# Loading w_down's last row of each partition by eight loads of four partitions

## The chip, the cores and the metric

The kernel runs on one core of a Trainium2 chip. The metric is the device time of one execution in microseconds (us). A core has engines that run side by side, each with its own queue of instructions: TensorE (PE; its weight loads are listed as PEld), VectorE (DVE), ScalarE (ACT), GpSimd (POOL) and SyncE (SP). In this kernel SP issues all transfers between device memory and the on-chip memory of 128 partitions; 16 DMA engines carry them out.

## What is computed

One decoding step of four sequences: attention over a cache of 4096 positions and 32 heads, a gated feed-forward net beside it, and a mix of the two by a gate. All of it is in float32.

```python
g = sigmoid((x * gate_w).sum(-1, keepdims=True))          # x: 4 x 1 x 512
q = x @ wq                                                # wq: 512 x 4096, 32 heads of 128
p = softmax(q @ k_cache.T * 128 ** -0.5)                  # k_cache: 4 x 32 x 4096 x 128
a = (p @ v_cache) @ wo                                    # wo: 4096 x 512
b = (gelu(x @ w_gate) * (x @ w_up)) @ w_down              # 512 x 1792, 512 x 1792, 1792 x 512
out = g * a + (1 - g) * b
```

The two caches are 256 MiB each, and nearly all of the kernel's traffic. wq and wo are 8192 KB each, w_gate, w_up and w_down 3584 KB each.

## The kernel before

**Stages.** At the start wq, x, the first K tile and gate_w are loaded, then w_gate and w_up. The queries are computed on PE. The loop over `i` in 0 to 31 then takes one K tile and one V tile a step: four heads of one sequence, 8192 KB each, 64 KB in each partition. DVE multiplies a K tile by the query (`products`, L213) and sums over the head's 128 elements (`sums`, L219), each in two parts: a quarter of the tile that is shared with its neighbour in memory first, and then the other three quarters. PE turns the maxima (L228, L235), ACT takes the exponentials (L240), and PE multiplies the result by V(i-1) (`pv`, L272). In step 0 the feed-forward net up to its hidden vector is computed as well: `ffn_up` on PE (L334), `ffn_gelu` on DVE and ACT (L341 to L346), and 14 transposes of 128 by 32 on DVE (L349) into `hT`. After the loop come `load_d` (w_down, one load, L88) and `load_w` twice (wo, two loads of 2048 KB for its first half and six of 1024, 1024, 768, 512, 512 and 256 KB for its second, L95). PE then runs the last `pv`, the product with w_down (`ffn_down`, 14 products through `project_wide`, L254), the first half of wo (also L254), the fold of `wide` into `acc` (L264, L259) and the second half of wo (L259, four products for each of 16 rows, as its pieces land). DVE copies the result (L413) and SP stores it (L414).

**Memory.** One tile `big` of 45056 floats in each partition holds everything large. Even K tiles are in columns 0 to 16383, odd ones in 12288 to 28671, so neighbours share a quarter. V tiles are in 28672 to 45055, the last one, V(31), in 0 to 16383. w_down is put in 36864 to 44031 and the first half of wo in 28672 to 36863, both once V(30) has been used by PE; the second half of wo is put in 16384 to 24575, once K(31) has been summed by DVE. The columns 24576 to 26623, also in K(31), serve small results (`ES`).

**Order.** The schedule is by hand: each engine executes its instructions in the order of the program text, and a framework adds the semaphores. SP's order near the end is K(31), V(30), V(31), w_down, then wo in eight pieces, then the store. An SP instruction that waits holds all that are behind it.

Of the kernel before, what the change touches and what calls it, by code (L numbers as in the profile page):

```python
# [9 lines left out]
F32 = mybir.dt.float32  # L10
# [7 lines left out]
def tile_gated_mix(ctx: ExitStack, tc: tile.TileContext, x, kc, vc, wq, wo, w_gate, w_up, w_down, gate_w, out):  # L18
    nc = tc.nc
    P = 128  # L20
    B, H, S, D = kc.shape
    DM = x.shape[2]
    F = w_gate.shape[1]
# [9 lines left out]
    RJ = 4  # L33
    BP = 2
    FG = F // 4
    FC = F // P
    HW = 16
    E = HW * D // P
    GW = HW // HT
# [12 lines left out]
    consts = ctx.enter_context(tc.tile_pool(name="consts", bufs=1))  # L52
# [9 lines left out]
    big = kv.tile([P, VA + TW], F32)  # L62
    Q0, F0, F1, W0, D0 = VA, VA, VA + KC * F, VA, VA + TW // 2
    W1, ES = TW, TW + TW // 2

    def place(a, n):
        return big[:, a:a + n]
# [17 lines left out]
        nc.sync.dma_start(place((F0, F1)[s], KC * F), (w_gate, w_up)[s].rearrange("(p c) n -> p (c n)", c=KC))  # L85

    def load_d():
        nc.sync.dma_start(place(D0, FC * DM), w_down.rearrange("(p i) n -> p (i n)", i=FC))  # L88

    def load_w(w):  # L90
        t = place((W0, W1)[w], E * DM)
# [152 lines left out]

    acc = ps1.tile([P, C4], F32, name="acc")
    wide = ps1.tile([P, DM], F32, name="wide")
    NW = FC + E
    nw = iter(range(NW))


    def project_wide(t, w):
        n = next(nw)
        c = n % 4
        nc.tensor.matmul(wide[32 * c:32 * c + 32, :], t, w, start=n < 4, stop=n >= NW - 4)  # L254

# [69 lines left out]


    hT = consts.tile([P, FC, 32], F32)
    fu = place(VA + 2 * KC * F, 2 * DM).rearrange("p (s n) -> p s n", s=2)

    def ffn_up(s):  # L330
# [7 lines left out]
    def ffn_gelu():  # L338
        x1 = fu[:, 0, :FG]
        t1, t2, t3, th, y, v = (place(F1 + a * DM, FG) for a in range(6))  # L340
        nc.vector.tensor_tensor(t1, x1, x1, op=OP.mult)  # L341
        nc.vector.tensor_scalar(t2, t1, 0.044715, 1.0, op0=OP.mult, op1=OP.add)
        nc.vector.tensor_tensor(t3, t2, x1, op=OP.mult)  # L343
        nc.scalar.activation(th, t3, AF.Tanh, scale=c_gelu)  # L344
        nc.vector.scalar_tensor_tensor(y, th, 1.0, x1, op0=OP.add, op1=OP.mult)  # L345
        nc.vector.scalar_tensor_tensor(v, y, half, fu[:, 1, :FG], op0=OP.mult, op1=OP.mult)  # L346

        for i in range(FC):
            nc.vector.transpose(hT[:, i, :], v[:, i::FC])  # L349

    def ffn_down():
        for f in range(FC):
            project_wide(hT[:, f, :], place(D0 + f * DM, DM))


    load_f(0)
# [2 lines left out]
    for i in range(NT):  # L359
# [12 lines left out]
        if i == 0:  # L372
            half, gmask = gates()
            ffn_up(0)
            ffn_up(1)
            ffn_gelu()
            load_v(0)
# [14 lines left out]
        if b == 1 and g + 1 < NG:  # L392
            q_spread(g + 1)
    load_d()
    load_w(0)
    load_w(1)
# [4 lines left out]
    gather(NG - 1)  # L401
    weigh(NG - 1)
    ffn_down()
    turn(1)
    turned(1)
# [31 lines left out]
```

## Time and profile before

| what | value |
|---|---|
| median of 3 runs (lowest, highest) | 1313.7 us (1313.62, 1313.85) |
| the profiled execution | 1313.51 us |
| its span in the profile | 1311.7 us |
| DVE busy | 1143.1 us, 87% |
| PE busy | 392.2 us, 30% |
| ACT busy | 92.6 us, 7% |
| mean granted clock of TensorE | 0.633 |

The profile covers one execution; what lies between its span and its time, 1.8 us, is ahead of the first instruction and behind the last. Rows have the start and the duration in microseconds, the engine, the source line and operation, and the tile written and the tiles read ("big<-in_A_wo" is a load of wo into `big`). SPq is SP's queue. In the chain of waits each row is a stretch of the work that ended last, followed back from the end; a stretch put down to a DMA runs from its issue, or from the end of the row before it, to its landing. In lists of waits the columns are the waiting engine and line, what it waited for, the sum, the number of waits and the longest. A wait for several things is put down to the one that the profile saw last. In rows by line, "|" is followed by the busy time and the mean duration in nanoseconds, and then by the idle time before. Rows of stretches give the bounds, the length, busy time and instructions of PE, PEld, DVE, ACT and POOL, then the granted clock, the share of the DMA engines' time and GB/s.

### The profile page before, as it was taken

To read this page: it belongs to the slowest core of one execution; us is meant where nothing else is said; L and a number is where in the kernel's file an instruction comes from. 1 tells how busy PE (TensorE), PEld (TensorE's weight loads), DVE (VectorE), ACT (ScalarE), POOL (GpSimd) and SP (SyncE) were. 2 spreads that over 40 slices of the span, in tenths; PEclk is the share of its full clock that TensorE was granted. 3 is DMA by queue.
4 is the path that set the end of the run, shared out by engine and by line. 5 is a ranking of instruction groups with operands and counts; after the bars stand their busy time and mean duration, and the time that the engine had idled before them with its cause. 6 is when DMAs were issued, how large, how long until landed. Compare 5 with 4: busy or idle time off the path is not lost.

```text
span 1311.7 us, 6366 instructions
## 1 busy us (share of the span) xinstructions
PE 392.2 (30%) x2728; PEld 131.1 (10%) x2728; DVE 1143.1 (87%) x261; ACT 92.6 (7%) x321; POOL 0.7 (0%) x6
## 2 busy tenths in 40 slices
PE   2403323322233221333232233322133333123237
PEld 0100001000010000100001000100001000010013
DVE  1899889988899988988989988998889898898890
ACT  0010000000000100000000000000000000000010
POOL 0000000000000000000000000000000000000000
PEclk9656666556666655666656666665566665566669
DMA  9999999999999999999999999999999999999998
GB/s 416 436 428 442 422 440 426 438 436 436 436 428 436 432 436 436 436 430 432 434 436 434 436 430 436 428 438 430 434 446 422 442 422 442 434 434 440 426 426 341
DMA packets 11143, 565.07 MB, mean 431 GB/s; under 512 B 1368, under 2 KB 1384, under 8 KB 1900
## 3 DMA queue, kind: packets, MB, share of 16 engines
q1 hardware_dynamic: 11116, 564.68, 99.5%
q8 instruction: 21, 0.34, 0.1%
q14 instruction: 6, 0.05, 0.0%
HBM read 564.67 MB, written 0.01 MB: 430 GB/s over the span
## 4 chain that ended last, share of the span: by engine, by line
DMA 73%; DVE 26%; issue 0%; PE 0%; SPq 0%; ACT 0%; DVEq 0%
DMA big<-in_A_k_cache 69%; DVE big L213 13%; DVE sc L219 13%; DMA big<-in_A_v_cache 2%; DMA big<-in_A_wo 2%; DVE m L233 0%; DVE hT L349 0%; PE acc L259 0%; DVE big L346 0%; DVE big L345 0%; DVE big L341 0%; DVE big L343 0%; ACT big L344 0%; DVE m L226 0%; DVE t L313 0%
## 5 line engine op out<-in xcount | busy, mean ns | idle before, releaser
L213 DVE TENSOR_TENSOR big<-big,qb 128x4096 f32<-128x4096 f32 x64 | 555.8, 8685 | 104.1 <-DMA big<-in_A_k_cache 104.1
L219 DVE TENSOR_REDUCE sc<-big 128x32 f32<-128x4096 f32 x64 | 555.4, 8678 | 1.1
L272 PE MATMUL po<-big,PM 128*32 128x512 f32 x2048 | 295.1, 741 | 437.2 <-DMA big<-in_A_v_cache 434.8
L272 PEld LDWEIGHTS po<-big,PM 128*32 128x32 f32 x2048 | 80.9, 133 | 625.2 <-issue 622.7
L235 PE MATMUL sm<-m,ones 1*128 1x4 f32 x64 | 18.7, 360 | 218.0 <-DVE m L233 218.0
L228 PE MATMUL sm<-ident,m 128*1 128x128 f32 x32 | 11.7, 365 | 214.5 <-DVE m L226 182.7
L240 ACT ACTIVATE PM<-sc,nb 32x128 f32<-32x128 f32 x128 | 67.3, 526 | 2.5
L237 ACT ACTIVATE nb<-sm 128x4 f32<-128x4 f32 x32 | 5.5, 173 | 570.3 <-PE sm L235 570.3
L235 PEld LDWEIGHTS sm<-m,ones 1*128 1x128 f32 x64 | 15.9, 306 | 237.7 <-DVE m L233 237.7
L281 ACT ACTIVATE o<-po 128x512 f32<-128x512 f32 x16 | 9.6, 597 | 324.8 <-PE po L272 324.8
L228 PEld LDWEIGHTS sm<-ident,m 128*1 128x1 f32 x32 | 2.5, 79 | 237.0 <-issue 185.9
L240 ACT ACTIVATION_READ_ACCUMULATOR PM<-sc,nb 32x1 f32 x128 | 26.2, 205 | 0.0
L200 ACT ACTIVATE qb<-q 128x512 f32<-128x512 f32 x8 | 4.8, 597 | 245.3 <-PE q L196 245.3
L128 DVE COPY xT<-sm 128x128 f32<-128x128 f32 x4 | 0.9, 284 | 20.6 <-PE sm L125 20.6
L196 PE MATMUL q<-QM,hmask 128*32 128x512 f32 x64 | 14.6, 1004 | 3.5 <-DVE QM L186 3.5
L289 PE MATMUL sm<-o,sel 128*16 128x128 f32 x128 | 15.6, 273 | 0.0
L334 PE MATMUL q<-big,xT 128*32 128x448 f32 x64 | 10.3, 810 | 9.4 <-DMA big<-in_B_w_gate 4.9
L299 DVE RECIPROCAL ri<-sm 16x1 f32<-16x1 f32 x8 | 1.2, 146 | 13.3 <-PE sm L291 13.3
L289 PEld LDWEIGHTS sm<-o,sel 128*16 128x16 f32 x128 | 11.8, 97 | 7.4 <-issue 5.0
L413 DVE COPY res<-acc 128x128 f32<-128x128 f32 x1 | 0.3, 291 | 12.7 <-PE acc L259 12.7
L226 DVE TENSOR_REDUCE m<-sc 128x1 f32<-128x128 f32 x32 | 9.2, 286 | 1.1
L233 DVE TENSOR_REDUCE m<-sm 1x4 f32<-1x128 f32 x32 | 8.7, 272 | 0.6 <-PE sm L228 0.6
(61 smaller groups left out, 77.1 us busy)
## 6 DMA issues: line engine op xcount, KB each, us to landing
big<-in_A_wo SPq DMA_DIRECT2D x2, 2048.0 KB, 27.0
big<-in_B_w_gate SPq DMA_DIRECT2D x1, 3584.0 KB, 21.4
big<-in_B_w_up SPq DMA_DIRECT2D x1, 3584.0 KB, 27.5
big<-in_B_w_down SPq DMA_DIRECT2D x1, 3584.0 KB, 18.0
big<-in_A_wo SPq DMA_DIRECT2D x2, 1024.0 KB, 24.6
big<-in_A_wo SPq DMA_DIRECT2D x2, 512.0 KB, 28.2
big<-in_A_wo SPq DMA_DIRECT2D x1, 768.0 KB, 28.0
big<-in_A_k_cache SPq DMA_DIRECT2D x32, 29.6
```

Source lines behind the costliest of these rows:

```text
L196: nc.tensor.matmul(ps[h * PH:(h + 1) * PH].rearrange("p b d -> p (b d)"), hmask[:, j, a:a + 1].to_broadcast([P, PH]), QM.rearrange("p b d ...
L213: nc.vector.tensor_tensor(t, t, QB[g][:, b:b + 1, :].to_broadcast([P, r1 - r0, D]), op=OP.mult)
L219: nc.vector.tensor_reduce(SC[i][:, r0:r1], K(i).rearrange("p (r d) -> p r d", d=D)[:, r0:r1], axis=AX.X, op=OP.add)
L226: nc.vector.tensor_reduce(m1, SC[i], axis=AX.X, op=OP.max)
L228: nc.tensor.transpose(MT[i], m1, ident)
L233: nc.vector.tensor_reduce(m2, MT[i].rearrange("o (h p) -> o h p", h=HT), axis=AX.X, op=OP.max)
L235: nc.tensor.matmul(nbp, ones[:1, :], m2, start=True, stop=True)
L240: nc.scalar.activation(PM[:, PZ:].rearrange("p (c m) -> p c m", m=32)[s, :, h:RJ * HT:HT], SC[i][s, :].rearrange("p (c j) -> p c j", j=RJ) ...
L272: nc.tensor.matmul(PO[i // BP % 2][32 * c:32 * c + 32].rearrange("p j d -> p (j d)"), PM[:, m0:m0 + 32], V(i)[:, j * N:(j + 1) * N], start ...
L281: nc.scalar.activation(O[i // BP], PO[i // BP % 2], AF.Copy)
L289: nc.tensor.matmul(OS[g][:, :D], sel[:, j, m0:m0 + B * HT], O[N * g + n][:, j, :], start=(n, j) == (0, 0), stop=(n, j) == (N - 1, RJ - 1))
L334: nc.tensor.matmul(ps[32 * j:32 * j + 32, :], xT[:, c, :32], place((F0, F1)[s] + c * F + j * FG, FG), start=c == 0, stop=c == KC - 1)
```

## The change

w_down's 1792 rows lie 14 to a partition. Thirteen of each partition's 14 are still loaded by one load, now into 6656 instead of 7168 columns. The last row of each of the 128 partitions, 128 rows of 2 KB in all, goes to partitions 0 to 31 instead, four rows to a partition, in columns 26624 to 28671 (`DX`), by eight loads. Load `p` writes the partitions p, p+8, p+16 and p+24 and carries 16 rows, 32 KB. The hidden vector is transposed to match: 13 transposes as before and four of 32 by 32 into `hX`. The product with w_down becomes 13 products over 128 partitions and four over 32. The numbers that are summed are the same.

```diff
-    FC = F // P
+    FR = F // P
+    FC = FR - 1
+    XP, XC = 32, P // 32
...
+    DX = ES + 4 * DM
...
     def load_d():
-        nc.sync.dma_start(place(D0, FC * DM), w_down.rearrange("(p i) n -> p (i n)", i=FC))
+        rows = w_down.rearrange("(p i) n -> p i n", i=FR)
+        nc.sync.dma_start(place(D0, FC * DM), rows[:, :FC].rearrange("p i n -> p (i n)"))
+        last = rows[:, FC].rearrange("(k a p) n -> p a k n", k=XC, p=8)
+        for p in range(8):
+            nc.sync.dma_start(place(DX, XC * DM)[p:XP:8].rearrange("a (k n) -> a k n", k=XC), last[p])
...
-    NW = FC + E
+    NW = FC + XC + E
...
     hT = consts.tile([P, FC, 32], F32)
+    hX = consts.tile([XP, XC, 32], F32)
...
         for i in range(FC):
-            nc.vector.transpose(hT[:, i, :], v[:, i::FC])
+            nc.vector.transpose(hT[:, i, :], v[:, i::FR])
+        for k in range(XC):
+            nc.vector.transpose(hX[:, k, :], v[k * XP:(k + 1) * XP, FC::FR])
...
     def ffn_down():
         for f in range(FC):
             project_wide(hT[:, f, :], place(D0 + f * DM, DM))
+        for f in range(XC):
+            project_wide(hX[:, f, :], place(DX + f * DM, DM)[:XP])
```

## The prediction

> **What bounds the kernel now.** I read the page's totals first, then the chain of waits in order of time, then the waits and the issue times of SyncE's DMA queue (SP) near the end.
>
> ```profile
> span 1311.7 us, 6366 instructions
> PE 392.2 (30%) x2728; PEld 131.1 (10%) x2728; DVE 1143.1 (87%) x261; ACT 92.6 (7%) x321; POOL 0.7 (0%) x6
> DMA  9999999999999999999999999999999999999998
> q8 instruction: 21, 0.34, 0.1%
> HBM read 564.67 MB, written 0.01 MB: 430 GB/s over the span
> big<-in_B_w_down SPq DMA_DIRECT2D x1, 3584.0 KB, 18.0
> ```
>
> The DMA engines are busy in every slice, VectorE (DVE) for 87%. The bytes set the time; what counts is whether the DMA queue ever runs empty. The chain shows the same, and its rhythm gives a price:
>
> ```profile
> 1202.71 4.42 DVE big L213
> ...
> 1241.31 4.42 DVE big L213
> ...
> 1250.28 29.67 DMA big<-in_A_v_cache
> ...
> 1279.97 27.61 DMA big<-in_A_wo
> ...
> 1307.62 1.08 PE acc L259 x24
> ...
> 1308.72 0.29 DVE res L413
> ```
>
> One step of the loop is 1241.31 - 1202.71 = 38.6 us for one K and one V load of 8192 KB each: 19.3 us for 8192 KB behind other loads. The last wait is for wo:
>
> ```profile
> 1308.23 0.16 PEld L259 LDWEIGHTS acc<-big 128*32 128x32 f32 x8 [0.23 <-DMA big<-in_A_wo]
> ```
>
> So the last piece of wo lands at 1308.2, and 3.5 us of work end the span. Every microsecond by which that landing moves is a microsecond of the kernel. Now the queue that issues these loads:
>
> ```profile
> SPq L95 <- DMA big<-in_B_w_down: 8.1, 1, 8.1
> SPq L95 <- DVE m L226: 4.8, 1, 4.8
> SPq L95 <- DMA big<-in_A_v_cache: 2.1, 1, 2.1
> 1270.41 0.33 SPq L88 DMA_DIRECT2D big<-in_B_w_down  x1
> 1270.79 0.43 SPq L95 DMA_DIRECT2D big<-in_A_wo  x1
> 1276.13 0.33 SPq L95 DMA_DIRECT2D big<-in_A_wo  x1
> 1279.97 0.33 SPq L95 DMA_DIRECT2D big<-in_A_wo  x1
> 1288.43 0.33 SPq L95 DMA_DIRECT2D big<-in_A_wo  x1
> ```
>
> After V(31) come w_down and eight pieces of wo. Neither of the last two pieces shares memory with what it waits for: the seventh waits for V(31), which lands at 1279.97, the eighth for w_down, which lands at 1288.43. In both cases the awaited load is the one eight places before it in the queue's order. I read this as a limit: each load reuses the completion counter of the load eight before it, and SP holds it, and everything behind it, until that one has landed. Today this costs nothing: seven of the eight pieces stand in the queue long before w_down lands, and only the last, 256 KB, comes late.
>
> **The change part by part.** *The queue.* Eight small loads (32 KB each, 256 KB together) now stand between w_down and wo. Their place is columns 26624 to 28671, the end of K(31). The sum at L219 reads that until
>
> ```profile
> 1263.15 12.95 DVE L219 TENSOR_REDUCE sc<-big 128x96 f32<-128x12288 f32 x1
> ```
>
> 1276.10, so the first small load goes out at 1276.1, where the third piece of wo goes out now (the 4.8 us wait above). The first two pieces of wo, issued from 1270.79 now, are held behind it. That alone would be free: V(31) and w_down keep the DMA engines fed until about 1287.8, and without this cover it would cost up to 1276.1 - 1270.8 = 5.3 us.
>
> The eight before are another matter. The seventh small load is eight places behind V(31) and waits until 1279.97. The eighth is eight places behind w_down and waits for its landing. All of wo stands behind that eighth load. So none of wo's 8192 KB can be issued until the last byte of everything before it has landed: the queue runs empty once. What is late next is wo's last landing, and with it the end.
>
> The price, step by step. w_down loses one row in 14, 256 KB; at 430 GB/s that is 262144 B / 430 GB/s = 0.6 us, so it lands at 1288.43 - 0.6 = 1287.8. The eighth small load is issued then. The trace has no load of its shape (4 partitions by 4 rows); the nearest rows are the load of x, of four partitions, and the store of the result, of four by four runs:
>
> ```profile
> L99 SPq DMA_DIRECT2D big<-in_A_x x1: 355/355/355, 1.2 to 1.2; - x1
> L414 SPq DMA_DIRECT2D out<-res x1: 661/661/661, 1309.0 to 1309.0; - x1
> L97 SPq DMA_DIRECT2D big<-in_A_wq x1: 388/388/388, 0.7 to 0.7; - x1
> DMA to landing us min/median/max: 21.9/21.9/21.9
> ```
>
> That is 0.36 to 0.66 us; I take 0.55, between them, and 0.05 to the next issue (1270.79 - 1270.41 - 0.33). The first piece of wo goes out at 1287.8 + 0.6 = 1288.4, within 1288.2 to 1288.5.
>
> What do 8192 KB take from issue to last landing when the queue is empty? The trace has exactly one such load, wq (512 x 4096 floats, 8192 KB), the kernel's first: 21.9 us, the last row above. That is 21.9 - 19.3 = 2.6 us more than behind other loads: start-up, refill and the last receipts. wo in eight pieces takes 1308.2 - 1288.4 = 19.8 us from w_down's landing now, 0.5 more than the loop's 19.3; whether that half microsecond comes again bounds wo at 21.9 to 22.4. I take 22.4, since the pieces stay as they are. wo's last landing: 1288.4 + 22.4 = 1310.8, that is +2.6 against 1308.2.
>
> The Trainium skill (DMA: Bandwidth & Descriptors, Anatomy of one DMA) gives a fixed cost of about 2.0 us per DMA, nearly all of it the receipt after the last byte, fitted on GpSimd's path. By that figure an empty queue would cost 2.0 instead of 2.6 and the sum would be smaller by 0.6; the trace's row is of this queue and this size, so it decides.
>
> One more term is small but not nothing. The page's queue q8 fetches instructions over the same DMA engines, 21 packets for 2728 + 2728 = 5456 TensorE instructions, or 260 instructions each.
>
> ```profile
> 590.98 30.69 DMA big<-in_A_k_cache
> ...
> 630.67 29.67 DMA big<-in_A_k_cache
> ...
> 1094.68 30.69 DMA big<-in_A_k_cache
> ...
> 1134.37 29.59 DMA big<-in_A_k_cache
> 1288.40:1308.20 19.80, 14.95 (x226) 7.55 (x221) 1.74 (x4) 1.82 (x3) 0.00 (x0) 1.00 0.87 365
> ```
>
> The tail has 226 + 221 = 447 of these, so one or two fetches. In the loop two K landings of some 29 come late, by 30.69 - 29.6 = 1.1 us. I estimate that a fetch delays the engine it strikes by up to this, and that in steady state most fetches strike an engine that is not the last. After an empty queue all engines start level, so a strike in wo's 20 us can count in full: 0 to 1.1, I take 0.5, about the middle.
>
> *VectorE.* Fourteen transposes become thirteen and four smaller ones:
>
> ```profile
> 68.46 1.71 DVE L349 STREAM_TRANSPOSE hT<-big 128x32 f32<-128x32 f32 x14
> 70.31 0.33 SPq L76 DMA_DIRECT2D big<-in_A_v_cache  x1
> 50.97 0.33 SPq L76 DMA_DIRECT2D big<-in_A_k_cache  x1
> DMA to landing us min/median/max: 25.8/29.6/40.4
> ```
>
> 1.71 / 14 = 0.12 each: +0.4 if a smaller one costs as much, -0.1 if next to nothing. They hold up V(0)'s issue at 70.31, but K(1), issued at 50.97 and landed at 50.97 + 25.8 = 76.8 at the earliest (the last row is the time from issue to landing of all K and V loads), still feeds the DMA engines. Nothing, or +0.4 if that cover were gone.
>
> *TensorE.* Fourteen products of w_down become seventeen, four of them over 32 partitions.
>
> ```profile
> L254 PE MATMUL wide<-big,hT 128*32 128x512 f32 x28 | 3.6, 595 | 0.0
> 1298.35 0.16 PEld L254 LDWEIGHTS wide<-big 128*32 128x32 f32 x8 [2.30 <-DMA big<-in_A_wo]
> ```
>
> 3.6 / 14 = 0.26 each at most, so +0.8, or +0.3 if a product over 32 partitions costs little. PE waits 2.3 us for wo right afterwards, which hides it; bare it would be +0.8. The last small load must be there too: issued at 1287.8, it lands within 2 us if the result's store is a guide (issued 1309.04, all over at 1311.7), while the products begin at 1290.4.
>
> The sum: wo's last landing -0.6 (smaller w_down) + 0.6 (issues) + 2.6 (empty queue) + 0.5 (a fetch) = **+3.1**; the rest is hidden. The profiled execution took 1313.51, of which the span is 1311.7; it lies 0.2 below the median of the runs, 1313.7. So 1316.6 for an execution like it and **1316.8** for the median. The bounds: 0.36 + 0.05 for the issues, 21.9 for wo, no fetch, gives 1310.1 and 1315.6; 0.71, 22.4 and 1.1 gives 1312.0 and 1317.5.
>
> **The rivals.** *A: no empty queue, not slower.* The two waits at L95 could be something other than a limit of eight in flight, such as an ordering by memory that I don't see. Then the eighth small load goes out at about 1280, wo follows from 1280.5, seven microseconds before the DMA engines are through, and the bytes are the same as before: 1313.7, or down to 1313.1 if the small loads run on DMA engines that are ahead of the others and only w_down's 0.6 shows. For it: such a limit stands nowhere in the kernel's text. Against it: two waits in a row, each on the load eight places before.
>
> *B: a quarter of the engines.* A load of four partitions may be carried by four DMA engines only. Then 256 KB at a quarter of 430 GB/s take 2.4 us on those four, which save 0.6 of w_down: +1.8 at wo's landing, without an empty queue: 1315.5. The Trainium skill (DMA: Bandwidth & Descriptors, Why a DMA increments its semaphore by 16 and not by 1) says so: the number of engines is the largest up to 16 that divides the slowest dimension, four here. No view of this profile tells the engines apart. With the empty queue this hides in it: seven of the loads are through in 7 x 0.3 = 2.1 us after w_down.
>
> *C: both.* If those four engines are also the last to finish w_down, they start wo up to 2.4 - 1.5 = 0.9 us after the others (1.5 being the gap, estimated as the 0.6 of issues and about 1 us to the first byte out of wq's 2.6): 1317.7.
>
> **How the numbers follow.** The forecast, 1315.6 to 1317.5, gets 0.75, C 0.10, A 0.08 and B 0.07. No change that this kernel's measurement could tell ends at 0.2%, 2.6 us: below 1311.1 or above 1316.3. About two thirds of the forecast's own range and C lie above: 0.75 x 0.68 + 0.10 = 0.61 slower. The rest of the forecast, A and B are within: 0.37. For faster, which none of the cases gives, 0.02. The range 1315.0 to 1318.2 leaves out A and a remainder.
>
> **What would show it.** The eighth small load and all eight pieces of wo issued after 1287.5, with a wait of SP on w_down of about 7 us at the new load's line; the slices or a window of 1284 to 1290 with a visible drop of the DMA share; wo's last landing near 1311.3. wo issued near 1280.5 would prove A or B. The forecast is wrong if the refill after an empty queue in mid-kernel costs much less than at the program's start, or if a fetch falls clear of wo.

## The result, and the profile after

The changed kernel takes 1324.22 us (median of 6 runs, 1323.33 to 1324.9) against 1313.7 before: 1.0079 times as long, with a 95% interval of 1.0066 to 1.0092. That is +10.5 us. The prediction was +3.1 and a range that ended at 1318.2. The profiled execution took 1323.63, its span is 1321.8, against 1313.51 and 1311.7.

The page's totals of the changed kernel hardly differ from those before; only the last slices of the DMA row do.

```profile
span 1321.8 us, 6396 instructions
PE 390.5 (30%) x2734; PEld 131.3 (10%) x2734; DVE 1143.9 (87%) x264; ACT 92.5 (7%) x321; POOL 0.7 (0%) x6
DMA  9999999999999999999999999999999999999986
```

The waits of SP's queue over the last 97 us (waiting line and what it waited for, sum, times, longest) and SP's own timeline there (start, duration):

```profile
SPq L97 <- DMA big<-in_B_w_down: 7.8, 1, 7.8
SPq L97 <- DVE m L235: 5.5, 1, 5.5
```

```profile
1270.99 0.33 SPq L94 DMA_DIRECT2D big<-in_B_w_down  x1
1276.49 13.31 SPq L97 DMA_DIRECT2D big<-in_B_w_down  x8
1289.85 3.98 SPq L104 DMA_DIRECT2D big<-in_A_wo  x8
```

This is the predicted step. The first small load goes out at 1276.49. The eighth waits 7.8 us for w_down and goes out at 1289.17 (the chain below). All eight pieces of wo follow from 1289.85 on. The DMA engines do run dry. The same stretch before and after (bounds, length, busy time and count of PE, PEld, DVE, ACT, POOL, granted clock, DMA share, GB/s), first the kernel before:

```profile
1284.00:1290.00 6.00, 6.00 (x61) 2.34 (x50) 0.00 (x0) 0.60 (x1) 0.00 (x0) 1.00 0.97 414
```

and the changed kernel:

```profile
1284.00:1290.00 6.00, 0.00 (x0) 0.00 (x0) 0.00 (x0) 0.00 (x0) 0.00 (x0) 0.50 0.36 121
1313.00:1319.00 6.00, 5.11 (x148) 3.78 (x140) 0.11 (x1) 0.60 (x1) 0.00 (x0) 1.00 0.01 3
```

The DMA share falls from 0.97 to 0.36. But the first row shows something else as well: TensorE, busy for all of these 6 us before, does nothing. And in the second row all loads are through by 1313, while TensorE works on for 6 us. The end no longer follows wo's landing. The chain of the changed kernel, in order of time, says what it follows (left out rows are marked by "..."):

```profile
1270.99 18.16 DMA big<-in_B_w_down
...
1289.17 2.54 DMA big<-in_B_w_down
...
1291.97 0.63 ACT big L329
1292.60 0.07 ACT nb L246
...
1294.90 8.37 PE po L281 x64
1303.27 1.77 PE sm L298 x16
...
1314.91 3.96 PE acc L268 x136
...
1318.89 0.29 DVE res L427
```

The eighth small load lands at 1291.71. Only then does ScalarE run L329, the copy of `spread(0)`, and behind it in its program order the softmax of the last tile and with it the last `pv`, the gather and everything that TensorE does to the end. ScalarE's timeline at that copy (in brackets the idle time before and who ended it), before:

```profile
1276.14 0.63 ACT L320 ACTIVATE big<-t 128x512 f32<-128x512 f32 x1 [27.18 <-DVE sc L219]
```

and after:

```profile
1291.97 0.63 ACT L329 ACTIVATE big<-t 128x512 f32<-128x512 f32 x1 [42.65 <-DMA big<-in_B_w_down]
```

Before, the copy waits for VectorE's last sum. After, it waits for the small loads, 15.8 us longer. The last `pv` starts at 1294.90; before, it started at 1280.35:

```profile
1280.35 8.39 PE L272 MATMUL po<-big,PM 128*32 128x512 f32 x64 [2.45 <-ACT PM L240]
```

The copy writes columns 24576 to 25087, the loads write 26624 to 28671: they share nothing. The order that the framework made of the program nevertheless lists all eight loads' counters ahead of the copy:

```
L329 Activation big<-t 128x512 [waits DMAHW4, DMAHW3, DMAHW5, DMAHW2, DMAHW6, DMAHW1, DMAHW7, DMAHW0, DVE]
```

From `pv` to the result's copy it is 24.0 us now (1318.89 - 1294.90). Before it was 28.4 (1308.72 - 1280.35), waits for wo included. So of `pv`'s delay of 14.55 us, 4.4 are absorbed by waits that are no longer there, and 10.2 remain: the change.

### The profile page after: what moved, and what is told of

It reads as the page before. It is cut to its first block, busy times and chain, and to the rows that moved or that the text cites. A ratio compares the mean times of both kernels' runs of the same rounds, so it can differ in the third digit from the quotient of the medians.

```text
span 1321.8 us, 6396 instructions
## 1 busy us (share of the span) xinstructions
PE 390.5 (30%) x2734; PEld 131.3 (10%) x2734; DVE 1143.9 (87%) x264; ACT 92.5 (7%) x321; POOL 0.7 (0%) x6
## 4 chain that ended last, share of the span: by engine, by line
DMA 73%; PE 23%; DVE 2%; issue 0%; ACT 0%; SPq 0%; ACTq 0%; DVEq 0%
DMA big<-in_A_v_cache 69%; PE po L281 22%; DMA big<-in_A_k_cache 3%; DMA big<-in_B_w_down 2%; DVE big L222 1%; PE wide L263 1%; DVE sc L228 0%; PE acc L268 0%; ACT PM L249 0%; PE sm L298 0%; DVE hT L359 0%; PE oT L316 0%; DVE hX L361 0%; DVE big L356 0%; DVE big L355 0%
## 5 line engine op out<-in xcount | busy, mean ns | idle before, releaser
L173 PE MATMUL po<-big,xT 128*32 128x512 f32 x64 | 9.0, 729 | 0.4 <-DVE xT L137 0.4
```

## The experiments

The theory from these rows: two costs, ScalarE held behind the small loads and the empty queue, of which the first sets the end and hides the second. The rival: the queue alone makes the end late, and ScalarE's wait is on the way. Each of the two costs was then taken away alone, then both.

**spread(0) ahead of the loads.** ScalarE's copy no longer waits for them.

```diff
+    spread(0)
     load_d()
     load_w(0)
     load_w(1)
-    spread(0)
```

> The changed kernel with the first spread(0) moved ahead of load_d, so that ScalarE's copy no longer waits for the eight small loads. Theory (two costs: ScalarE held behind the small loads, which sets the end now at a span of 1321.8; behind it the empty DMA queue, whose last wo landing is at 1313.2): the softmax of the last tile starts near 1278 again, TensorE's last pv near 1280, and the end follows wo's last landing: 1313.2 + 3.5 = a span of 1316.7, a time of 1318.5. Rival (the late end comes from the DMA queue alone, ScalarE's wait only shows it): no change, 1324.2.

Measured: 1318.73 us, 1.0039 (1.0025 to 1.0052). Its chain ends as the kernel's before did, in loads:

```profile
1270.65 18.15 DMA big<-in_B_w_down
...
1288.82 0.63 SPq L97
...
1289.49 0.44 SPq L104
...
1292.49 19.80 DMA big<-in_A_wo
...
1312.34 1.55 PE acc L268 x24
...
1313.91 0.29 DVE res L427
```

The copy runs at 1276.34, `pv` at 1280.55, and the end follows wo. What is left is the cost of the empty queue, +5.0 us, with a slower end on TensorE in it (see below). The rival falls. The edit does not remove the wait between the two, it turns it round: SP's first small load now waits for the copy and goes out at 1276.99, half a microsecond later. That costs nothing here, since the eighth waits for w_down anyway.

```profile
SPq L97 <- ACT big L329: 6.0, 1, 6.0
```

**Four loads of eight partitions.** With four loads between w_down and wo, the first three pieces of wo have no wait for w_down. ScalarE's wait stays.

```diff
-        last = rows[:, FC].rearrange("(k a p) n -> p a k n", k=XC, p=8)
-        for p in range(8):
-            nc.sync.dma_start(place(DX, XC * DM)[p:XP:8].rearrange("a (k n) -> a k n", k=XC), last[p])
+        last = rows[:, FC].rearrange("(k a p) n -> p a k n", k=XC, p=4)
+        for p in range(4):
+            nc.sync.dma_start(place(DX, XC * DM)[p:XP:4].rearrange("a (k n) -> a k n", k=XC), last[p])
```

> The changed kernel with four small loads of eight partitions four apart instead of eight of four. No load stands eight places behind w_down until wo's fourth piece, so the queue does not run empty; ScalarE's copy still waits for the small loads. Theory (two costs): the four land at 1286 to 1288.5, and from the last small landing to the end of the span the changed kernel takes 1321.8 - 1291.7 = 30.1, so a span of 1316.1 to 1318.6, a time of 1318 to 1320.4, set by TensorE, with wo's last landing back near 1308. Rival (the queue alone): 1313.1 to 1313.7.

Measured: 1321.54 us, 1.0057 (1.0042 to 1.0072). The stretch of 1284 to 1290 is full again, and ScalarE still late:

```profile
1284.00:1290.00 6.00, 0.00 (x0) 0.00 (x0) 0.00 (x0) 0.81 (x3) 0.00 (x0) 0.50 1.03 438
```

```profile
1278.54 10.47 DMA big<-in_B_w_down
...
1289.16 0.63 ACT big L329
...
1292.09 9.07 PE po L281 x64
```

The last of the four lands at 1289.01, `pv` starts at 1292.09. It ended 1.1 us above what I had expected: the landing is half a microsecond later than the latest that I allowed, and `pv` takes 9.07 instead of 8.37. ScalarE's wait alone costs 7.8 us.

**Both edits.**

> Both edits together: four small loads and spread(0) ahead of load_d. Theory (two costs and no third): both are gone, wo's last landing is at 1308.2 or 0.6 earlier, a time of 1313.1 to 1313.7. A third cost, such as the strided small writes slowing w_down or the smaller products on TensorE, would leave it above 1314.2.

Measured: 1313.95 us (1313.12 to 1314.7), 1.0001 (0.9992 to 1.001): the time before. No third cost is left in this form, so the smaller transposes and products are hidden as predicted. Alone the two cost 5.0 and 7.8 us, together 10.5 and not 12.8, since the late `pv` and the late wo partly pass side by side.

**Number of loads or number of partitions?** The four loads differ from the eight in both. Starting from the kernel with both edits, each of the four was cut in two: eight loads, each still of eight partitions.

```diff
         for p in range(4):
-            nc.sync.dma_start(place(DX, XC * DM)[p:XP:4].rearrange("a (k n) -> a k n", k=XC), last[p])
+            for r in range(0, XC, 2):
+                nc.sync.dma_start(place(DX + r * DM, 2 * DM)[p:XP:4].rearrange("a (k n) -> a k n", k=2), last[p][:, r:r + 2])
```

> The run with four strided loads and spread(0) first, each of its four loads cut in two (two of the four rows each): eight small loads again, but each still of eight partitions, the same bytes in the same places. Theory (the number of loads between w_down and wo empties the queue, since the eighth waits for w_down): 1318.7 as in the run with spread(0) first and eight loads of four partitions; all of wo issued after w_down's landing. Rival (the four-partition loads themselves cost the time, by using few DMA engines): 1313.95 as with four loads.

Measured: 1318.03 us, 1.0031 (1.002 to 1.0043).

```profile
SPq L98 <- DMA big<-in_B_w_down: 6.0, 1, 6.0
```

```profile
1276.83 11.89 SPq L98 DMA_DIRECT2D big<-in_B_w_down  x8
1288.76 4.00 SPq L105 DMA_DIRECT2D big<-in_A_wo  x8
```

The same bytes in the same places cost 4.1 us more as eight loads than as four. It is the number of loads that makes nearly all of the queue's cost; the 0.7 us between this run and the first one, with eight loads of four partitions and spread(0) first, are taken up below.

**Adjacent partitions, eight loads.** Does ScalarE wait because of where the loads write, or of how?

```diff
-        last = rows[:, FC].rearrange("(k a p) n -> p a k n", k=XC, p=8)
+        last = rows[:, FC].rearrange("(k p a) n -> p a k n", k=XC, p=8)
         for p in range(8):
-            nc.sync.dma_start(place(DX, XC * DM)[p:XP:8].rearrange("a (k n) -> a k n", k=XC), last[p])
+            nc.sync.dma_start(place(DX, XC * DM)[4 * p:4 * p + 4].rearrange("a (k n) -> a k n", k=XC), last[p])
```

> The changed kernel with its eight small loads going to four adjacent partitions each instead of four eight apart; nothing else moved. In this form the framework makes ScalarE's spread(0) wait for none of them. Theory (ScalarE's wait comes from the strided form, not from any shared columns): pv starts near 1280 as in the run with spread(0) first, the empty queue stays, 1318.7; if writes of several DMA engines into neighbouring partitions hinder each other, as the one-load run (1316.1 instead of 1313.5 to 1314.2) makes likely, up to 3 us more, 1321.7. Rival (ScalarE waits because the columns lie near each other): 1324.

Measured: 1318.32 us, 1.0033 (1.002 to 1.0045).

```profile
1276.54 0.63 ACT L329 ACTIVATE big<-t 128x512 f32<-128x512 f32 x1 [27.18 <-DVE sc L228]
```

The columns are the same, `spread(0)` is where it was, and ScalarE doesn't wait. So the wait comes from the strided form of the load. That the framework takes this form to touch what the copy writes is the likely reading; the runs show the wait, not the rule. What is left is the empty queue again, +4.5.

**One load, and four adjacent ones.** Two more forms without either cost: one load for all 128 rows to 32 partitions, and four loads of eight adjacent partitions.

```diff
-        last = rows[:, FC].rearrange("(k a p) n -> p a k n", k=XC, p=8)
-        for p in range(8):
-            nc.sync.dma_start(place(DX, XC * DM)[p:XP:8].rearrange("a (k n) -> a k n", k=XC), last[p])
+        last = rows[:, FC].rearrange("(k p) n -> p k n", k=XC)
+        nc.sync.dma_start(place(DX, XC * DM)[:XP].rearrange("p (k n) -> p k n", k=XC), last)
```

> The changed kernel with one load for all of the last rows, 32 partitions of four rows, adjacent partitions; spread(0) stays behind it. The order that the framework makes for this form has no wait of ScalarE on the load. Theory: neither cost is left and all sixteen DMA engines carry the 256 KB, 1313.5 to 1314.2. If instead the place of the small loads in the queue or the 32-partition products cost something by themselves, above 1314.5.

```diff
-        last = rows[:, FC].rearrange("(k a p) n -> p a k n", k=XC, p=8)
-        for p in range(8):
-            nc.sync.dma_start(place(DX, XC * DM)[p:XP:8].rearrange("a (k n) -> a k n", k=XC), last[p])
+        last = rows[:, FC].rearrange("(k p a) n -> p a k n", k=XC, p=4)
+        for p in range(4):
+            nc.sync.dma_start(place(DX, XC * DM)[8 * p:8 * p + 8].rearrange("a (k n) -> a k n", k=XC), last[p])
```

> Four small loads of eight adjacent partitions each; spread(0) not moved, no wait of ScalarE on them, no empty queue. If only the two costs exist: 1313.1 to 1314.2, like the run with four strided loads and spread(0) first (1313.95). If neighbouring partitions hinder each other's writes: 1315 to 1316.5, like the one load.

Measured: 1316.07 us, 1.0017 (1.0009 to 1.0026), for the one load, where I had expected the time before; 1316.76 us, 1.0019 (1.001 to 1.0029; the runs from 1315.15 to 1317.2), for the four, just above the second of the two cases that I had given. There is a third cost in these forms. The same stretch of the one-load kernel:

```profile
1284.00:1290.00 6.00, 6.00 (x52) 1.65 (x45) 0.00 (x0) 0.00 (x0) 0.00 (x0) 0.84 1.04 319
```

of the four adjacent loads:

```profile
1284.00:1290.00 6.00, 6.00 (x56) 1.84 (x49) 0.00 (x0) 0.12 (x1) 0.00 (x0) 0.91 1.02 311
```

and of the four strided loads with spread(0) first:

```profile
1284.00:1290.00 6.00, 6.00 (x52) 1.57 (x48) 0.00 (x0) 0.00 (x0) 0.00 (x0) 0.83 1.00 424
```

All three keep the DMA engines busy, but the first two move 319 and 311 GB/s in it, the third 424. w_down shows where the time goes. It stands behind V(31) in the queue, so the time is taken from V(31)'s issue to the issue of SP that waits for w_down's landing, in each run's profiled execution:

| small loads | V(31) issued | w_down awaited until | between |
|---|---|---|---|
| none (the kernel before) | 1250.28 | 1288.43 | 38.15 |
| four strided, eight partitions each | 1250.34 | 1287.83 | 37.5 |
| the same, spread(0) first | 1251.27 | 1288.80 | 37.5 |
| eight halves of these, spread(0) first | 1250.32 | 1288.04 | 37.7 |
| eight adjacent, four partitions each | 1250.68 | 1288.31 | 37.6 |
| eight strided, four partitions each, spread(0) first | 1250.48 | 1288.82 | 38.3 |
| eight strided, four partitions each (the changed kernel) | 1250.64 | 1289.17 | 38.5 |
| one, 32 partitions | 1250.60 | 1289.57 | 39.0 |
| four adjacent, eight partitions each | 1250.46 | 1290.14 | 39.7 |

w_down is shorter by 0.6 us at 430 GB/s, which leaves 37.55. Four forms come to that. The one load and the four adjacent ones are 1.4 and 2.1 us above it: w_down itself lands late. Why is open. That neighbouring partitions hinder each other's writes, as I had supposed, isn't enough as a reason: the eight adjacent loads go to neighbours too, and w_down isn't late with them.

**Two rows moved.** In the run with both edits w_down, with 1/14 less in it, comes to 37.5 us in the table above instead of 38.15. Two rows, each by four strided loads, one group ahead of w_down, might shorten the last engines' work further. The lines left out of the diff also let spread(0) write into the space of `xT`, so that ScalarE waits for none of the loads, and let the result share a buffer with `tm`.

```diff
-    FC = FR - 1
+    FC = FR - 2
...
-    DX = ES + 4 * DM
+    DX = (D0 + FC * DM, ES + 4 * DM)
...
+        for x in range(2):
+            last = rows[:, FC + x].rearrange("(k a p) n -> p a k n", k=XC, p=4)
+            if x == 1:
+                nc.sync.dma_start(place(D0, FC * DM), rows[:, :FC].rearrange("p i n -> p (i n)"))
+            for p in range(4):
+                nc.sync.dma_start(place(DX[x], XC * DM)[p:XP:4].rearrange("a (k n) -> a k n", k=XC), last[p])
...
```

> A version that may beat both: two of w_down's 14 rows of each partition go to partitions 0 to 31, each by four loads of eight partitions four apart, one group ahead of w_down (columns 43008 to 45055), one behind it; spread(0) writes into the space of xT, so ScalarE waits for none of them, and the result shares a buffer with tm. Theory (the last DMA engines are not those that carry the small loads; each row moved takes 0.6 us from them, as w_down's 7.9 us from V(31)'s landing in the four-load runs against 8.5 before shows): wo's last landing 1.2 earlier, 1312.5. If the engines are level at the end, the eight that carry more finish last: 1.2 later, 1314.9.

Measured: 1315.15 us (1313.74 to 1315.69), 1.0008 (0.9999 to 1.0017). It beats neither the kernel before nor the version with both edits. Its median is near the rival's 1314.9, that the engines that carry more then finish last. No view tells the engines apart, and the profiled execution is the fastest of the eleven (1313.74, with the result's copy at 1308.63 against 1308.72 before), so this isn't settled. I found no version that is faster than the kernel before.

## Why the prediction was wrong

**The step that failed** is the premise that "every microsecond by which that landing moves is a microsecond of the kernel", with "the rest is hidden" in the sum. It held for what waits behind the new loads on SP's queue, which I followed instruction by instruction. Of the last small load I asked only when TensorE's products need it ("The last small load must be there too", at 1290.4), not which instruction of another engine would wait for it. ScalarE's `spread(0)` does, it stands ahead of the last softmax, and 24 us of TensorE's work hang on that. The copy and the loads share a tile but no columns, so the prediction's reading of who uses the loads' columns could not find it; the adjacent and the strided form of the same load show that the form decides. The load's time was off too: 2.54 us from issue to landing, where I had put "within 2 us". This step cost 10.5 - 5.0 = 5.5 us on top of the empty queue.

**The queue's step was right in its mechanism.** A load waits for the load eight places before it; the eighth small load holds all of wo behind w_down; the DMA share falls. Eight loads against four of the same bytes prove the count. **Its size was off:** +3.1 predicted, 5.0 measured with spread(0) first (4.5 with the eight adjacent loads and 4.2 with the eight halves, which have it alone too). In the run with spread(0) first the result's copy starts at 1313.91 against 1308.72, 5.2 later, 2.1 more than the sum. By the terms:

- w_down's landing was put at 1287.8; it is 1288.80, 1.0 later. The 0.6 saved is there in four of the forms in the table, and not with eight strided loads of four partitions, which come to 38.3 and 38.5. Why these take it back is open.
- The issues were put at 0.6; the eighth load takes 0.63 and the next issue comes at 1289.49, 0.67 in all.
- From wo's first issue to the result's copy I had 22.4 + 0.5 + 0.5 (the last from 1308.2 to 1308.72) = 23.4; it is 1313.91 - 1289.49 = 24.4. Half of this 1.0 is not wo: TensorE's last 24 products take 1.55 instead of 1.08, at half the granted clock, although the 1.08 includes a wait of 0.23 for the last piece. The prediction took the work behind the last landing as unchanged. The stretch from the start of these products to the result's copy, with spread(0) first and then in the kernel before:

```profile
1312.34:1313.91 1.57, 1.51 (x24) 0.99 (x24) 0.00 (x0) 0.00 (x0) 0.00 (x0) 0.50 0.01 3
1307.62:1308.72 1.10, 1.03 (x24) 0.53 (x24) 0.00 (x0) 0.00 (x0) 0.00 (x0) 1.00 0.02 6
```

  Without these 0.47 the 24.4 would be 23.95, at the upper bound of 24.0 that allowed for a fetch of 1.1. The halves and the eight adjacent loads have the same 1.55 and come to 24.2 and 24.1 without the 0.47. What part of the rest is the fetch and what the refill stays open, and so does what brought the clock down: the one-load kernel, whose queue isn't empty, has the same 1.55 at 0.50.

**VectorE and TensorE.** The four smaller transposes take 0.22 each, more than the 0.12 of the large ones; V(0) is issued at 71.07, 0.76 later than before, against the 0.4 that I allowed. The four products over 32 partitions take 1.06 in all, near my upper bound. Both are hidden, as the 1313.95 with both edits shows.

**The rivals.** A (no empty queue) is refuted by SP's timeline. B (the quarter of the engines is the cost) is refuted as the main cost by the eight halves, which with eight partitions cost 4.2 of the 5.0. C (both) is open: the 0.7 us by which eight strided loads of four partitions are slower than the halves is near its 0.9, but the eight adjacent loads, also of four partitions, don't hold w_down up (37.6 in the table). None of them was the ScalarE wait, and all three went by SP's queue: the range came out too narrow because every case in it ended with wo's landing.

## What to carry to other kernels

For each load that is added, list who waits for it on every engine, in the order that the framework really made, and what stands behind that wait; that two accesses share no bytes did not keep them apart here when one of them had a stride over partitions. Count the loads between two large ones as well as their bytes: where each reuses the counter of the eighth before, eight small loads emptied a queue that four left full. Before a load is split over few partitions, compare GB/s and not only the DMA engines' busy share.

## What the runs showed that I had not expected

An issue of a small strided load holds SP for about twice as long as one to adjacent partitions, four rows each. The changed kernel and the one with adjacent partitions:

```profile
L97 SPq DMA_DIRECT2D big<-in_B_w_down x8: 629/630/800, 1276.5 to 1289.2; - x8
```

```profile
L97 SPq DMA_DIRECT2D big<-in_B_w_down x8: 250/296/302, 1276.5 to 1288.3; - x8
```

And a DMA share of 1.04 went with 319 GB/s: a full share in these rows is no proof of full speed.
